# Counting TensorE's instructions in the planner: runs of 96 small products instead of 192, and 12 opening zero products instead of 50

## The chip, the cores and the metric

The kernel runs on one core of one Trainium2 chip. The metric is the device time in microseconds (us), taken as the median of timed runs. The core's engines work from queues of their own: TensorE (PE: matmuls, and PEld: its weight loads), VectorE (DVE), ScalarE (ACT), GpSimd (POOL) and SyncE (SP, which here issues nearly all DMAs). An instruction waits on its queue for the results that it needs, and what stands behind it in the same queue waits too.

## The reference

Two things are computed, one after the other. First a linear attention with a decaying state, step by step over 768 tokens, for 4 batches × 8 heads of width 48:

```python
for t in range(S):
    cur = einsum('bhd,bhe->bhde', u * k[t], v[t])
    y[:, :, t] = einsum('bhd,bhde->bhe', r[t], state + cur)
    state = w[t][..., None] * state + einsum('bhd,bhe->bhde', k[t], v[t])
```

Then a two-layer network on the 3072 × 384 matrix x made of y: h = x @ w_in (384 to 2048), g = h where h >= 1, 0 where h <= -1, (h + 1)² / 4 between, and out = g @ w_out (2048 to 384). All in float32.

## The kernel before, in words

**The network.** The 3072 tokens are cut into 6 blocks of 512 (`WIDE`), and the 2048 hidden columns into 16 groups f of 128. A step is one block and one f. `product_in` (matmuls at line 1272) makes h from x in nine matmuls of 512 columns: three row blocks, each as high × high, high × low and low × high part of numbers split into two float32r halves. The gate follows: Relu and Square on ACT (lines 1084 and 1085), min and max on DVE (1086), the high half on ACT (1088), the low half on DVE (1089). `product_out` (line 1292), nine matmuls again, adds the result into three PSUM banks. h takes one of two spare PSUM banks (`SPARE`, an operation with `grab` takes one, the one that names it in `drop` gives it back). Blocks 0 and 1 start with half steps of 256 columns (`HALVES`), because x of their second half comes later. The last block goes another way (`fast`, matmuls at line 984) that isn't touched.

**The weights** arrive as raw words, one f at a time, and are decoded by ACT (lines 441, 445, 447), POOL or DVE (449) and DVE (451, 454). Line 454 finishes the low half of one f.

**The attention** is done in 12 units u of 64 tokens of every batch, two units to a block. For each, DVE runs a scan forward and one backward over the decays (514 and 509) and scales r and k (585, 535). Then PE issues small products of 64 rows, 64 columns or so, in stretches:
- `among` (line 555): 32 matmuls, r with k inside the unit, one stretch more with u for u < 3; DVE masks the result (561).
- `ktrans` (594): 4 transposes for each of two halves of k, copied by ACT (603).
- `cross` (667): 16 matmuls, r with the old state; u = 0 has none. It holds a spare bank in units 1 to 10, in which the second half of umat is written.
- `umat` (624): 32 matmuls, k with v; DVE makes the new state of it (640, 642, 645).
- `along` (667): the other 16 of r with the state and 32 of the inner part with v, into the same two banks as cross. ACT and DVE then move y out as x in two halves (739, 741); in units 0 and 1 over a spreading product (`spread`, 760).

A float32 matmul of this kind is issued in two passes, each a weight load and a matmul, so one call is four instructions and two matmul records; a float32r one is two instructions and one record.

**The order** of all engines is written out by a planner, class `Plan`. Each operation is added with its engine, cost in us, due time and what it reads and writes. `order` is a list scheduler: it takes the engine that can go first, and on it the ready operation with the smallest key. A result is seen by another engine `HOP` later. `late` runs the same backwards from the end and gives keys; `best` tries 40 orders with shaken keys (`SHAKES`, fixed seed) and keeps the one with the earliest modelled end. `glue` ties operations of PE into a run that nothing may part. `kept_warm` puts products with a tile of zeros (`zeros`, line 403) into pauses of PE that the model sees in the opening. `warm` (line 409) opens PE's queue with `WARM` small zero products, each over one quarter of the array.

The lines that matter most here, from the function `attention`:

```python
run.append(op("PE", 0.6 if glued else 0.8, ..., cross, fresh=not alone, grab=glued))
if glued:
    run.append(multiplied())            # umat
run.append(op("PE", (1.6 if glued else 1.74) if u else 1.27, ..., along, fresh=False))
if glued:
    plan.glue(*run)
```

So in units 1 to 10 (`glued`) cross, umat and along stand in one run. Unit 11 has no umat and isn't glued; unit 0 has no cross.

Of the kernel before, what the change touches and what calls it, by code (L numbers as in the profile page):

```python
# [41 lines left out]
LAG = 2  # L42

FAST = {NB - 1}

WARM = 50

# [15 lines left out]
class Plan:  # L63
# [13 lines left out]
    def add(self, engine, cost, emit, due, reads=(), writes=(), port=False, size=0, fresh=True, first=None, grab=False, uses=(), drop=None):  # L77
# [9 lines left out]
        self.ops.append(dict(e=engine, cost=cost, emit=emit, due=due, deps=deps, port=port, size=size,  # L87
                             fresh=fresh and engine == "PE", touch={*reads, *writes}, first=first, grab=grab, drop=drop, then=None,
                             uses={n} if grab else {*uses, *(() if drop is None else (drop,))}))
        return n  # L90
# [45 lines left out]
    def late(self):  # L136

        ops = self.ops
        users, left = [[] for _ in ops], [0] * len(ops)
        deps = [op["deps"] | {self.extra[n]} if n in self.extra else op["deps"] for n, op in enumerate(ops)]  # L140
        for n in range(len(ops)):
            for m in deps[n]:
                users[m].append(n)
                left[m] += 1
        free, back, since, open_, port = {}, {}, {}, {}, 0.0

        def opened(n):
            op = ops[n]
            since[n] = max((back[m] + (0.0 if ops[m]["e"] == op["e"] and not op["size"] else self.HOP) for m in users[n]), default=0.0)
            since[n] += self.end[n] - self.begin[n] - op["cost"]  # L150
            open_.setdefault(op["e"], []).append(n)

        def ready(n):
            return max(since[n], port) if ops[n]["port"] else since[n]

        for n, k in enumerate(left):
            if not k:
                opened(n)
        while any(open_.values()):
            t, e = min((max(free.get(e, 0.0), min(ready(n) for n in ns)), e) for e, ns in open_.items() if ns)  # L160
            n = max((n for n in open_[e] if ready(n) <= t + 1e-9), key=lambda n: (self.end[n], n))
            open_[e].remove(n)
            back[n] = free[e] = t + ops[n]["cost"]
            if ops[n]["port"]:
                port = back[n]
# [37 lines left out]
    def order(self):  # L203
# [12 lines left out]
        def opened(n):  # L216
            op = ops[n]
            since[n] = max((end[m] + (0.0 if ops[m]["e"] == op["e"] and not ops[m]["size"] else self.HOP) for m in op["deps"]), default=0.0)
# [16 lines left out]
        while any(open_.values()):  # L235
# [27 lines left out]
            begin[n] = t  # L263
            free[e] = end[n] = t + op["cost"] * (2 if e == "PE" and t < RISES else 1)
            if op["port"]:
                port = end[n]
                first.clear()
# [4 lines left out]
            if op["drop"] is not None:  # L272
                spare.append((end[n] + self.HOP, given[op["drop"]], n))
                first["PE"] = None
# [49 lines left out]
def attention_moe(tc, a):  # L324
# [81 lines left out]
    def warm():  # L406
        for n in range(WARM):
            r, c = n % 2 * 64, n // 2 % 2 * 64
            PE.matmul(hp[n % 2][c : c + 64, 0:32], lhsT=zero[r : r + 64, 0:64], rhs=zero[r : r + 64, 0:32], start=True, stop=True)

# [58 lines left out]
    def attention(u, when):  # L469
# [96 lines left out]
        if early:  # L566
            bd = [take(), take()]
            op("PE", 1.27, due, [("ku", 0), ("ku", 1), "nk", *both], [("b", bd[0]), ("b", bd[1])],
               lambda: among(bd, lambda q: ku[:, q]))
            for h in range(2):  # L570
# [19 lines left out]
        def ktrans(q, b):  # L590
# [5 lines left out]
        op("PE", 1.27, due, [("k", slot[0]), ("k", slot[1]), *both], [("b", ba[0]), ("b", ba[1])],  # L596
           lambda: among(ba, lambda q: rk[slot[q]][:, 1]))
        goes_on = u < NU - 1
        for q in (1, 0):
            if goes_on:  # L600
                b = take()
                op("PE", 0.4, due, [("k", slot[q]), "cst"], [("b", b)], lambda q=q, b=b: ktrans(q, b))
                op("ACT", 0.6, due, [("b", b)], [("kt", q)], lambda q=q, b=b: A.copy(
# [45 lines left out]
        def multiplied():  # L649
            return op("PE", 0.94 if glued else 1.27, due, [("kt", 0), ("kt", 1), vk], ukeys, umat, uses=lent.values())  # L650

        def stepped():
            for g in range(2):
                op("DVE", 0.5, due, [ukeys[g], ("ptot", u, 0), ("ptot", u, 1)] + ([("s", old, g)] if u else []), [("s", new, g)],
                   lambda g=g: step(g), drop=lent[0] if glued and g else None)
                if u:
                    op("DVE", 0.47, due, [("ptot", u, 0), ("ptot", u, 1)], [("s", new, g)], lambda g=g: fade(g), port=True)

# [48 lines left out]
        if u:  # L707
            run.append(op("PE", 0.6 if glued else 0.8, due, ss + [vk, ("r", slot[0]), ("r", slot[1])], [("b", by[0]), ("b", by[1])], cross, fresh=not alone,
                          grab=glued))
# [12 lines left out]
        if goes_on:  # L722
            stepped()
# [39 lines left out]
        if alone:  # L763
# [4 lines left out]
            for g in range(2):  # L768
                op("PE", 0.65, due, [("last_f", g), "perm", "nk", "ob"], [("b", by[g])], lambda g=g: spread(g), fresh=False)
        for what in (0,) if alone else (1, 0):  # L770
# [154 lines left out]
    def fast(n, after=()):  # L925
# [13 lines left out]
        hk = op("PE", 2.15, due, [("wh", f), ("wl", f), *xs, *after], [("h", n)],  # L939
                lambda: product_in(nc, bank[plan.given[hk]], f, x[:, 0], x[:, 1], w_hi, w_lo), grab=True)  # L940
        c = 0.6
# [46 lines left out]
        def multiply(late, reads, todo, fresh=False):  # L988
            banks = {("b", PLACE[to][0]): 0 for to, _, _ in todo}
            op("PE", 0.358 * len(todo), (n, -late * STEP - 0.1), reads, list(banks), lambda: accumulate(todo), fresh=fresh)  # L990

# [68 lines left out]
    def products(n, after=()):  # L1060
# [14 lines left out]
        for half in range(2):  # L1075
            if cs.start <= half * UT < cs.stop:
# [3 lines left out]
        step_ops.append(len(plan.ops))  # L1080
        hk = op("PE", 2.15 * k, due, [("wh", f), ("wl", f), *xs, *after], [("h", n)],
                lambda: product_in(nc, hs(), f, x[:, 0, :, cs], x[:, 1, :, cs], w_hi, w_lo), grab=True)
        c = 0.17 + 0.43 * k
# [4 lines left out]
        op("ACT", c, due, [("g", gk)], [("gh", gk)], lambda: nc.scalar.copy(ghs, gs))  # L1088
        op("DVE", 0.15 + 0.5 * k, due, [("g", gk), ("gh", gk)], [("gl", gk)], lambda: nc.vector.tensor_tensor(  # L1089
            out=gls, in0=gs, in1=ghs.bitcast(F32), op=ALU.subtract), port=True)  # L1090
# [5 lines left out]
        def second(n, f, ghs, gls, gk, terms, order=()):  # L1096
            op("PE", 2.15 * k * len(terms) / 9, (n, -LAG * STEP * k), [("gh", gk), ("gl", gk), ("wh", f), ("wl", f)],
               [*({("b", 3 + j): 0 for _, j in terms}), *order], fresh=begin,
               emit=lambda stop=end: product_out(nc, [x[:, cs] for x in acc], f, ghs, gls, w_hi, w_lo, begin, stop, terms))
# [262 lines left out]
```

## Time and profile before

| | us |
|---|---|
| timed runs | 511.04, 511.78, 512.08 |
| median | 511.78 |
| the profiled execution's own time | 510.8 |
| its span (first to last instruction) | 509.2 |
| PE busy in it | 486.8 |
| DVE busy | 367.0 |
| ACT busy | 305.6 |
| POOL busy | 97.0 |
| mean granted TensorE clock | 0.994 |

The profile is of one execution. Its page gives busy times and shares of each engine, the busy share in 40 equal slices of the span (a digit is tenths), the costliest groups of instructions, and DMA queues with packets and megabytes. The list of waits says who waited for whom: us in total, how often, the longest. "issue" there is idle time in which the engine waited for nothing that the profile shows. A row of the timeline has the start in us, the length in us, the engine, the line, the operation, output<-inputs, the shapes, how many instructions are merged in it, and in brackets the idle time of the engine before it and what ended it. A row of the table by stretches gives the stretch, its length, and the busy us of PE, PEld, DVE, ACT and POOL with the number of instructions of each.

### The profile page before, as it was taken

How to read it: one execution, taken by the hardware profiler on the slowest of the kernel's cores; microseconds unless marked ns; L12 is line 12 of the kernel's file. 1: busy time of each engine (PE TensorE's matmuls, PEld its weight loads, DVE VectorE, ACT ScalarE, POOL GpSimd, SP SyncE). 2: the span in 40 equal slices, each digit the busy share in tenths (PEclk: the TensorE clock that was granted, in tenths of full speed). 3: DMA queues.
4: the chain of work that ended last, by engine and by line, in shares of the span. 5: the costliest groups of instructions: out<-in, count | busy, mean ns of one | idle time of the engine just before them, and what ended most of it. 6: DMA issues, size and time to landing. Idle time of an engine off the chain costs nothing. (4 is left out here: it accounts for less than half of the span.)

```text
span 509.2 us, 13264 instructions
## 1 busy us (share of the span) xinstructions
PE 486.8 (96%) x5583; PEld 414.9 (81%) x5583; DVE 367.0 (72%) x631; ACT 305.6 (60%) x628; POOL 97.0 (19%) x80
## 2 busy tenths in 40 slices
PE   7778999999999999998999999999999999999994
PEld 5568988888889998877888887878878878889894
DVE  6899899988798888697963377854248544596653
ACT  4577979888866656565454556454365445575550
POOL 1654414411111111123010010200002402402000
PEclk9899999999999999999999999999999999999998
DMA  8977546245633350444320132400102000010002
GB/s 302 407 277 261 209 149 235 64 126 185 203 126 137 114 173 21 147 130 154 104 84 0 63 131 84 132 1 0 63 1 59 0 1 17 19 45 1 3 0 69
DMA packets 22052, 54.72 MB, mean 107 GB/s; under 512 B 3040, under 2 KB 9184, under 8 KB 21984
## 3 DMA queue, kind: packets, MB, share of 16 engines
q1 hardware_dynamic: 21840, 53.65, 30.6%
q8 instruction: 46, 0.75, 0.6%
q14 instruction: 22, 0.18, 0.1%
q10 hardware_dynamic: 144, 0.13, 0.1%
HBM read 47.09 MB, written 4.72 MB: 102 GB/s over the span
## 5 line engine op out<-in xcount | busy, mean ns | idle before, releaser
L1272 PE MATMUL h<-x,wt 128*128 128x512 f32 (+1 forms) x1035 | 219.4, 359 | 1.8 <-DVE x L739 1.5
L1272 PEld LDWEIGHTS h<-x,wt 128*128 128x128 f32 x1035 | 170.0, 188 | 32.5 <-DVE x L739 1.7
L1292 PE MATMUL acc<-gh,wt 128*128 128x512 f32 (+1 forms) x594 | 129.5, 353 | 0.0
L1292 PEld LDWEIGHTS acc<-gh,wt 128*128 128x128 f32 x594 | 97.6, 188 | 17.0
L1086 DVE SCALAR_TENSOR_TENSOR g<-g,h 128x512 f32<-128x512 f32 (+1 forms) x99 | 57.2, 578 | 70.2 <-ACT g L1085 69.9
L1084 ACT ACTIVATE g<-h 128x512 f32<-128x512 f32 (+1 forms) x99 | 50.9, 515 | 79.0 <-PE h L1272 68.0
L1292 PE MATMUL acc<-gl,wt 128*128 128x512 f32 (+1 forms) x297 | 72.1, 351 | 0.0
L1089 DVE TENSOR_TENSOR gl<-g,gh 128x512 fp32r<-128x512 f32 (+1 forms) x99 | 62.6, 642 | 7.8 <-ACT gh L1088 6.6
L1088 ACT CAST gh<-g 128x512 fp32r<-128x512 f32 (+1 forms) x99 | 52.5, 532 | 17.6 <-DVE g L1086 10.1
L1292 PEld LDWEIGHTS acc<-gl,wt 128*128 128x128 f32 x297 | 50.3, 188 | 8.4
L1085 ACT ACTIVATE g<-g 128x512 f32<-128x512 f32 (+1 forms) x99 | 54.5, 551 | 2.9
L581 POOL TENSOR_TENSOR r<-cst,d 128x512 f32<-128x512 f32 x18 | 19.7, 1113 | 168.5 <-PE bank L667 102.6
L449 POOL TENSOR_SCALAR wraw<-fl 128x768 uint16<-128x768 f32 x13 | 40.0, 3084 | 54.6 <-ACT wraw L447 54.6
L514 DVE TENSOR_TENSOR_SCAN p<-wq,seeds 128x520 f32<-128x520 f32 x24 | 32.3, 1346 | 3.2 <-DMA wq<-in_w 2.4
L573 POOL TENSOR_TENSOR nk<-nk 128x768 f32<-128x768 f32 x9 | 17.3, 1927 | 84.1 <-DMA nk<-in_nk 84.1
L509 DVE TENSOR_TENSOR_SCAN y<-wq,seeds 128x520 f32<-128x520 f32 x24 | 30.5, 1269 | 0.8
L945 DVE SCALAR_TENSOR_TENSOR rk<-rk,h 128x512 f32<-128x512 f32 x16 | 11.0, 687 | 18.3 <-ACT rk L944 18.0
L667 PE MATMUL bank<-r,vn 64*64 64x64 f32 (+1 forms) x768 | 15.4, 223 | 9.1 <-issue 9.1
L667 PEld LDWEIGHTS bank<-r,vn 64*64 64x64 f32 (+1 forms) x768 | 13.5, 135 | 9.9 <-issue 9.9
L942 ACT ACTIVATE rk<-h 128x512 f32<-128x512 f32 x16 | 9.6, 598 | 17.9 <-PE h L1272 17.7
L741 ACT CAST x<-bank 128x384 fp32r<-128x384 f32 x24 | 11.3, 485 | 12.3 <-PE bank L667 11.3
L561 DVE COPY_PREDICATED r<-below,bank 128x512 f32<-128x512 int32 x23 | 16.1, 734 | 3.3 <-PE bank L555 3.3
(198 smaller groups left out, 614.3 us busy)
## 6 DMA issues: line engine op xcount, KB each, us to landing
rk<-in_rk SPq DMA_DIRECT2D x24, 512.0 KB, 4.4
wraw<-in_wbits SPq DMA_DIRECT2D x16, 768.0 KB, 7.1
nk<-in_nk SPq DMA_DIRECT2D x9, 768.0 KB, 4.6
wq<-in_w SPq DMA_DIRECT2D x24, 260.5 KB, 3.0
vn<-in_v SPq DMA_DIRECT2D x12, 384.0 KB, 6.9
fl<-in_w SPq DMA_DIRECT2D x12, 260.0 KB, 2.9
out_y<-g SPq DMA_DIRECT2D x10, 256.0 KB, 2.6
x<-last SPq DMA_DIRECT2D x60, 32.0 KB, 2.5
```

Of the source, the lines that this page charges most:

```text
L449: op(on, 0.62 if f in SIGNS else 3.2, due, [("fl", k)], [("raw", f)], lambda: e.tensor_scalar(out=half(1), in0=s, scalar1=0.0, scalar2=327 ...
L509: V.tensor_tensor_scan(out=y_[:, ::-1], data0=w[:, SEG:0:-1], data1=sv[:, ::-1], initial=0.0, op0=ALU.mult, op1=ALU.add)
L514: V.tensor_tensor_scan(out=pv[:, q].rearrange("p n c -> p (n c)"), data0=w[:, 0:SEG], data1=sv, initial=0.0, op0=ALU.mult, op1=ALU.add,)
L581: op("POOL", 1.1, due, ["d", "cst"], [("R", h)], lambda h=h: G.tensor_tensor(out=r_[h], in0=twice.unsqueeze(1).unsqueeze(1).broadcast_to([ ...
L667: PE.matmul(out=bank[by[g]][HP * half : HP * half + M, lo : lo + C], start=first, stop=False, skip_group_check=True, **kw)
L1084: op("ACT", c, due, [("h", n)], [("g", gk)], lambda: nc.scalar.activation(gs, hs(), AF.Relu, scale=0.5, bias=0.5), uses=[hk])
L1085: op("ACT", c, due, (), [("g", gk)], lambda: nc.scalar.activation(gs, gs, AF.Square))
L1086: op("DVE", 0.13 + 0.53 * k, due, [("h", n)], [("g", gk)], lambda: nc.vector.scalar_tensor_tensor(out=gs, in0=gs, scalar=1.0, in1=hs(), op ...
L1088: op("ACT", c, due, [("g", gk)], [("gh", gk)], lambda: nc.scalar.copy(ghs, gs))
L1089: op("DVE", 0.15 + 0.5 * k, due, [("g", gk), ("gh", gk)], [("gl", gk)], lambda: nc.vector.tensor_tensor(out=gls, in0=gs, in1=ghs.bitcast(F ...
L1272: nc.tensor.matmul(hp, lhsT=wx[f][:, cs], rhs=xt[:, j, :], start=n == 0, stop=n == 8)
L1292: nc.tensor.matmul(o[j], lhsT=wx[f][:, cs], rhs=gt, start=first and i == 0, stop=stop and i == 2, skip_group_check=True)
```

## The change

The planner's model of the machine is made finer and gets a count of PE's instructions.
- Operations of PE carry `code`, the number of their instructions: 128 for among and umat, 64 for cross, 192 for along (128 in unit 0), 8 for ktrans, 12 for spread, 18 for a product. In `order`, `issued` keeps how many instructions PE has been given and when. An operation with more than 64 may start only so that its last instruction comes `FETCH` = 3.9 us after the one that stands `BLOCK` = 256 before it.
- cross and umat are still glued, along is not: it is an operation of its own that other products may precede. The state's DVE operations are added ahead of along.
- `after` replaces the single `HOP`: 0.2 us behind PE, 0.12 behind DVE and ACT, 0.15 behind POOL and SP; on ACT an instruction may begin 0.03 before the one ahead ends. Several costs are set anew.
- `warm` issues 12 zero products of 128 columns instead of 50 of 32.

What is computed for the output is the same; the order of the instructions is worked out anew by the same search.

```diff
-WARM = 50
+WARM = 12
...
     HOP = 0.15
+    HOPS = {"PE": 0.2, "DVE": 0.12, "ACT": 0.12, "POOL": 0.15, "SP": 0.15}
+    OVERLAP = {"ACT": 0.03}
+    BLOCK, FETCH = 256, 3.9
+
+    def after(self, m, n):
+
+        a, b = self.ops[m], self.ops[n]
+        if a["e"] == b["e"] and not a["size"]:
+            return 0.03 if a["e"] in self.OVERLAP else 0.0
+        return self.HOPS[a["e"]]
...
+        issued = [(0, -99.0, 0.0)]
+
+        def fetched(code):
+            at = issued[-1][0] + code - self.BLOCK
+            for had, t, each in reversed(issued):
+                if had <= at:
+                    return t + (at - had) * each + self.FETCH
+            return 0.0
+
...
+            if ops[n]["code"] > 64:
+                t = max(t, fetched(ops[n]["code"]) - ops[n]["cost"])
...
+            if e == "PE":
+                had = issued[-1][0]
+                if op["code"]:
+                    issued[-1] = had, t, op["cost"] / op["code"]
+                    issued.append((had + op["code"], t + op["cost"], 0.0))
+                first["PE"] = None
...
-            free[e] = end[n] = t + op["cost"] * (2 if e == "PE" and t < RISES else 1)
+            end[n] = t + op["cost"] * (2 if e == "PE" and t < RISES else 1)
+            free[e] = end[n] - self.OVERLAP.get(e, 0.0)
...
-            PE.matmul(hp[n % 2][c : c + 64, 0:32], lhsT=zero[r : r + 64, 0:64], rhs=zero[r : r + 64, 0:32], start=True, stop=True)
+            PE.matmul(hp[n % 2][c : c + 64, 0:128], lhsT=zero[r : r + 64, 0:64], rhs=zero[r : r + 64, 0:128], start=True, stop=True)
...
-            return op("PE", 0.94 if glued else 1.27, due, [("kt", 0), ("kt", 1), vk], ukeys, umat, uses=lent.values())
+            return op("PE", 1.07 if glued else 1.27, due, [("kt", 0), ("kt", 1), vk], ukeys, umat, uses=lent.values(), code=128)
...
-                op("ACT", 0.35, due, [("b", by[g])], [("look", g)], lambda g=g: A.copy(look[0:1, g : g + 1], bank[by[g]][0:1, 0:1]))
+                op("ACT", 0.15, due, [("b", by[g])], [("look", g)], lambda g=g: A.copy(look[0:1, g : g + 1], bank[by[g]][0:1, 0:1]))
         if glued:
-            run.append(multiplied())
-        run.append(op("PE", (1.6 if glued else 1.74) if u else 1.27, due, ss + [("R", 0), ("R", 1), vk, ("r", slot[0]), ("r", slot[1])],
-                      [("b", by[0]), ("b", by[1])], along, fresh=False))
-        if glued:
-            plan.glue(*run)
-        elif goes_on:
+            plan.glue(*run, multiplied())
+            stepped()
+        op("PE", 1.74 if u else 1.27, due, ss + [("R", 0), ("R", 1), vk, ("r", slot[0]), ("r", slot[1])],
+           [("b", by[0]), ("b", by[1])], along, fresh=False, code=192 if u else 128)
+        if goes_on and not glued:
             multiplied()
-        if goes_on:
             stepped()
```

In the same way the costs of cross (0.6 to 0.64), of the state's steps (0.5 to 0.55 and 0.47 to 0.57), of the products (2.15 to 2.1) and of a few others are set anew.

More of the change, by code (lines that the diff above doesn't have):

```diff
@@ L75, in __init__, with add @@
         self.given, self.extra = {}, {}
-    def add(self, engine, cost, emit, due, reads=(), writes=(), port=False, size=0, fresh=True, first=None, grab=False, uses=(), drop=None):
+    def add(self, engine, cost, emit, due, reads=(), writes=(), port=False, size=0, fresh=True, first=None, grab=False, uses=(), drop=None, code=0):
         deps = {self.writer[x] for x in (*reads, *writes) if x in self.writer}
@@ L87, in add @@
         self.ops.append(dict(e=engine, cost=cost, emit=emit, due=due, deps=deps, port=port, size=size,
-                             fresh=fresh and engine == "PE", touch={*reads, *writes}, first=first, grab=grab, drop=drop, then=None,
+                             fresh=fresh and engine == "PE", touch={*reads, *writes}, first=first, grab=grab, drop=drop, then=None, code=code,
                              uses={n} if grab else {*uses, *(() if drop is None else (drop,))}))
@@ L148, in opened @@
             op = ops[n]
-            since[n] = max((back[m] + (0.0 if ops[m]["e"] == op["e"] and not op["size"] else self.HOP) for m in users[n]), default=0.0)
+            since[n] = max((back[m] + self.after(n, m) for m in users[n]), default=0.0)
             since[n] += self.end[n] - self.begin[n] - op["cost"]
@@ L162, in late @@
             open_[e].remove(n)
-            back[n] = free[e] = t + ops[n]["cost"]
+            back[n] = t + ops[n]["cost"]
+            free[e] = back[n] - self.OVERLAP.get(e, 0.0)
             if ops[n]["port"]:
-                port = back[n]
+                port = free[e]
             for m in deps[n]:
@@ L217, in opened @@
             op = ops[n]
-            since[n] = max((end[m] + (0.0 if ops[m]["e"] == op["e"] and not ops[m]["size"] else self.HOP) for m in op["deps"]), default=0.0)
+            since[n] = max((end[m] + self.after(m, n) for m in op["deps"]), default=0.0)
             open_.setdefault(op["e"], []).append(n)
         forced, given, extra = {}, {}, {}
+        issued = [(0, -99.0, 0.0)]
[5 more added lines that the diff above has]
+            return 0.0
         spare = [(0.0, b, None) for b in SPARE]
@@ L263, in order @@
             begin[n] = t
-            free[e] = end[n] = t + op["cost"] * (2 if e == "PE" and t < RISES else 1)
+            end[n] = t + op["cost"] * (2 if e == "PE" and t < RISES else 1)
+            free[e] = end[n] - self.OVERLAP.get(e, 0.0)
             if op["port"]:
-                port = end[n]
+                port = free[e]
                 first.clear()
@@ L272, in order @@
             if op["drop"] is not None:
-                spare.append((end[n] + self.HOP, given[op["drop"]], n))
+                spare.append((end[n] + self.HOPS[e], given[op["drop"]], n))
                 first["PE"] = None
@@ L649, in multiplied @@
         def multiplied():
[L650 removed]
+            return op("PE", 1.07 if glued else 1.27, due, [("kt", 0), ("kt", 1), vk], ukeys, umat, uses=lent.values(), code=128)
         def stepped():
             for g in range(2):
[L654 removed]
+                op("DVE", 0.55, due, [ukeys[g], ("ptot", u, 0), ("ptot", u, 1)] + ([("s", old, g)] if u else []), [("s", new, g)],
                    lambda g=g: step(g), drop=lent[0] if glued and g else None)
                 if u:
[L657 removed]
+                    op("DVE", 0.57, due, [("ptot", u, 0), ("ptot", u, 1)], [("s", new, g)], lambda g=g: fade(g), port=True)
         begun = set()
@@ L707, in attention @@
         if u:
-            run.append(op("PE", 0.6 if glued else 0.8, due, ss + [vk, ("r", slot[0]), ("r", slot[1])], [("b", by[0]), ("b", by[1])], cross, fresh=not alone,
-                          grab=glued))
+            run.append(op("PE", 0.64 if glued else 0.8, due, ss + [vk, ("r", slot[0]), ("r", slot[1])], [("b", by[0]), ("b", by[1])], cross, fresh=not alone,
+                          grab=glued, code=64))
             if glued:
@@ L938, in fast @@
         step_ops.append(len(plan.ops))
-        hk = op("PE", 2.15, due, [("wh", f), ("wl", f), *xs, *after], [("h", n)],
-                lambda: product_in(nc, bank[plan.given[hk]], f, x[:, 0], x[:, 1], w_hi, w_lo), grab=True)
+        hk = op("PE", 2.1, due, [("wh", f), ("wl", f), *xs, *after], [("h", n)],
+                lambda: product_in(nc, bank[plan.given[hk]], f, x[:, 0], x[:, 1], w_hi, w_lo), grab=True, code=18)
         c = 0.6
@@ L989, in multiply @@
             banks = {("b", PLACE[to][0]): 0 for to, _, _ in todo}
-            op("PE", 0.358 * len(todo), (n, -late * STEP - 0.1), reads, list(banks), lambda: accumulate(todo), fresh=fresh)
+            op("PE", 0.351 * len(todo), (n, -late * STEP - 0.1), reads, list(banks), lambda: accumulate(todo), fresh=fresh, code=6 * len(todo))
         n0, f0, f1 = n - odd, f - odd, f - odd + 1
@@ L1080, in products @@
         step_ops.append(len(plan.ops))
-        hk = op("PE", 2.15 * k, due, [("wh", f), ("wl", f), *xs, *after], [("h", n)],
-                lambda: product_in(nc, hs(), f, x[:, 0, :, cs], x[:, 1, :, cs], w_hi, w_lo), grab=True)
+        hk = op("PE", 2.1 * k, due, [("wh", f), ("wl", f), *xs, *after], [("h", n)],
+                lambda: product_in(nc, hs(), f, x[:, 0, :, cs], x[:, 1, :, cs], w_hi, w_lo), grab=True, code=18)
         c = 0.17 + 0.43 * k
@@ L1088, in products @@
         op("ACT", c, due, [("g", gk)], [("gh", gk)], lambda: nc.scalar.copy(ghs, gs))
-        op("DVE", 0.15 + 0.5 * k, due, [("g", gk), ("gh", gk)], [("gl", gk)], lambda: nc.vector.tensor_tensor(
+        op("DVE", 0.17 + 0.54 * k, due, [("g", gk), ("gh", gk)], [("gl", gk)], lambda: nc.vector.tensor_tensor(
             out=gls, in0=gs, in1=ghs.bitcast(F32), op=ALU.subtract), port=True)
@@ L1096, in second @@
         def second(n, f, ghs, gls, gk, terms, order=()):
-            op("PE", 2.15 * k * len(terms) / 9, (n, -LAG * STEP * k), [("gh", gk), ("gl", gk), ("wh", f), ("wl", f)],
-               [*({("b", 3 + j): 0 for _, j in terms}), *order], fresh=begin,
+            op("PE", 2.1 * k * len(terms) / 9, (n, -LAG * STEP * k), [("gh", gk), ("gl", gk), ("wh", f), ("wl", f)],
+               [*({("b", 3 + j): 0 for _, j in terms}), *order], fresh=begin, code=2 * len(terms),
                emit=lambda stop=end: product_out(nc, [x[:, cs] for x in acc], f, ghs, gls, w_hi, w_lo, begin, stop, terms))
```

8 lines of the change are left out of this document (4 added, 4 removed).

## The prediction

> **What bounds the kernel now.** I read the page first, then the waits of TensorE (PE), then PE's timeline around each wait.
>
> ```profile
> span 509.2 us, 13264 instructions
> PE 486.8 (96%) x5583; PEld 414.9 (81%) x5583; DVE 367.0 (72%) x631; ACT 305.6 (60%) x628; POOL 97.0 (19%) x80
> PE   7778999999999999998999999999999999999994
> DVE  6899899988798888697963377854248544596653
> PEclk9899999999999999999999999999999999999998
> q8 instruction: 46, 0.75, 0.6%
> ```
>
> PE is busy for 96% of the span; from the fifth slice on (51 us) it is close to full, so from there time is won only by shortening PE's own row. PE idles 509.2 − 486.8 = 22.4 us. The two rows of the 40 slices show a second limit: in slices 3 to 9 VectorE (DVE) is at 8 or 9 tenths too. What PE waits for:
>
> ```profile
> PE bank L667 <- issue: 9.1, 6, 2.7
> PE h L409 <- POOL zero L388: 2.8, 1, 2.8
> PE h L1272 <- DVE x L739: 1.5, 1, 1.5
> ```
>
> The largest entry waits for no engine and no DMA: six pauses, "issue", all at line 667, the products that write y. In the order of time they are these (the bracket is the idle time before the row; x is the number of matmuls left after the pause):
>
> ```profile
> 18.98 1.10 PE L667 MATMUL bank<-r,vn 64*48 64x64 f32 x30 [2.67 <-issue]
> 41.69 0.67 PE L667 MATMUL bank<-r,vn 64*48 64x64 f32 x33 [1.70 <-issue]
> 71.84 0.57 PE L667 MATMUL bank<-r,vn 64*64 64x64 f32 x21 [1.09 <-issue]
> 128.44 0.50 PE L667 MATMUL bank<-r,vn 64*64 64x64 f32 x18 [1.16 <-issue]
> 151.46 0.75 PE L667 MATMUL bank<-r,vn 64*64 64x64 f32 x37 [0.93 <-issue]
> 240.03 0.56 PE L667 MATMUL bank<-r,vn 64*64 64x64 f32 x19 [1.53 <-issue]
> ```
>
> They belong to units u = 0, 1, 2, 3, 4 and 7. A unit from 1 to 10 issues cross, umat and along as one run of 32 + 64 + 96 = 192 matmul records; each record has a weight load of its own (5583 of both on the page), so 384 instructions. Here is u = 7, which pauses, and then u = 8, which doesn't:
>
> ```profile
> 235.72 0.69 PE L667 MATMUL bank<-rk,st 64*64 64x64 f32 x32
> 237.16 0.66 PE L667 MATMUL bank<-rk,st 64*64 64x64 f32 x32
> 237.64 0.87 PE L667 MATMUL bank<-r,vn 64*64 64x64 f32 x45
> ...
> 293.22 0.70 PE L667 MATMUL bank<-rk,st 64*64 64x64 f32 x32
> 293.74 0.20 PE L624 MATMUL bank<-vn,kt 64*64 64x48 f32 x1
> 294.66 0.66 PE L667 MATMUL bank<-rk,st 64*64 64x64 f32 x32
> 295.14 1.11 PE L667 MATMUL bank<-r,vn 64*64 64x64 f32 x64
> 296.18 1.66 PE L1292 MATMUL acc<-gh,wt 128*128 128x512 f32 x6
> ```
>
> I read the pause as instructions that have not arrived. The instruction queue row has 46 packets for 0.75 MB, about 16 KB each, and 2 × 5583 = 11166 PE instructions over 46 packets are some 243 each, so one packet carries about 256 instructions of 64 bytes. In u = 7 the pause follows 32 + 64 + 32 + 45 = 173 records; 256 instructions (128 records) before the first one that is late is the 13th or so of the 64 umat records, which by even spacing ran at about 236.4. From there to 240.03 are 3.6 us. A block that lies wholly in a run is used up in about 2 us (192 records take 296.18 − 293.22 = 2.96 us), and the next one is late. A run of 384 can hold a whole block or miss it: (384 − 256) / 256 is a half, and 5 of the 10 long runs pause.
>
> [...]
>
> **The change part by part.**
>
> *Long run cut in two (u = 1 to 10).* cross + umat stays glued, 192 instructions; along, again 192, may start only when the planner's count has its last instruction fetched: 256 back in the count plus 3.9 us. Right behind umat that is 1.8 us or so after umat's end, so the planner puts a product between, 2.10 us (the plain pitch of nine records, below). The tightest block then holds 46 instructions of umat, the product's 18 and all of along: about 0.3 + 2.2 + 1.5 = 4.0 us, longer than the 3.6 measured. I take all five pauses as gone: 1.70 + 1.09 + 1.16 + 0.93 + 1.53 = **−6.41 us**. Lower bound of the gain: 0, if they move elsewhere.
>
> *What the cut costs.* Unit 11 already issues its cross apart from its along, so its rows price it, against a plain product and against u = 8 above:
>
> ```profile
> 99.75 1.56 PE L1292 MATMUL acc<-gh,wt 128*128 128x512 f32 x6
> 101.85 0.39 PE L1272 MATMUL h<-x,wt 128*128 128x512 f32 x1
> ...
> 418.00 0.69 PE L667 MATMUL bank<-rk,st 64*64 64x64 f32 x32
> 418.62 2.36 PE L1272 MATMUL h<-x,wt 128*128 128x512 f32 x9
> 420.82 1.56 PE L1292 MATMUL acc<-gh,wt 128*128 128x512 f32 x6
> 423.01 0.69 PE L667 MATMUL bank<-rk,st 64*64 64x64 f32 x32
> 424.57 1.66 PE L1292 MATMUL acc<-gh,wt 128*128 128x512 f32 x6
> ```
>
> A plain product takes 2.10; the one after the small group 420.82 − 418.62 = 2.20, the one before it 423.01 − 420.82 = 2.19. cross alone lasts 0.62 against 293.74 − 293.22 = 0.52, along alone 1.56 against 296.18 − 294.66 = 1.52. Together 0.10 + 0.09 + 0.10 + 0.04 = 0.33 us for a cut, and ten of them are **+3.3 us**. Where along comes to stand beside another small product the cost is less; bounds 1.5 to 3.3, and I take 3.3 because unit 11 is the same step.
>
> *u = 0 and the opening zeros.* The opening zeros go from 50 × 2 records to 12 × 2, (100 − 24) × 2 = 152 instructions less, which moves every later block border back against the work. The 2.67 us pause came after 34 of along's 64 records; 152 instructions further on lies behind the end of along, so I take it as gone, and the planner's count also holds along back until its block is there. What does that win?
>
> ```profile
> 20.12 0.43 ACT L765 COPY ob<-bank 128x128 f32<-128x128 f32 x2 [3.98 <-PE bank L667]
> 23.26 1.01 DVE L454 TENSOR_TENSOR wt<-fl,wt 128x768 fp32r<-128x768 f32 x1 [0.61 <-ACT wt L441]
> 26.54 1.01 DVE L739 TENSOR_TENSOR x<-bank,x 128x384 fp32r<-128x384 f32 x2
> ```
>
> ScalarE (ACT) waited 3.98 us for along, but DVE, which must give x and the first weights before the first product, lost only 0.61 us to it, and at 26.54 it took x up without waiting. So **−0.6 us**; bounds 0 and −2.7. That the 24 zeros of 128 columns take another time than the 100 of 32 costs nothing: a 3.2 us stretch of filling zeros stands behind them. [...]
>
> ```profile
> 5.69 3.23 PE L403 MATMUL bank<-zero 128*128 128x512 f32 x6
> ```
>
> *Costs and hops in the planner* (0.2 behind PE, 0.12 behind DVE and ACT, ACT overlapping 0.03, the look copies 0.15 for 0.35) move no instruction by themselves; they make a new order out of the same search. I price them at 0, bounds −1.5 and +1.5, the size of a pause.
>
> *How much of the early gain reaches the end.* Up to 105 us the terms are −0.6, −(1.70 − 0.33) and −(1.09 − 0.33), together −2.7. But there DVE has no room:
>
> ```profile
> 75.00:102.00 27.00, 27.00 (x122) 21.91 (x121) 26.20 (x38) 24.37 (x39) 12.35 (x4) 1.00 0.45 160
> 87.15 4.36 PE L1272 MATMUL h<-x,wt 128*128 128x512 f32 x18
> 86.26 0.93 DVE L454 TENSOR_TENSOR wt<-fl,wt 128x768 fp32r<-128x768 f32 x1
> 102.00:500.00 398.00, 393.74 (x4164) 336.20 (x4163) 271.75 (x489) 227.10 (x484) 52.97 (x52) 1.00 0.23 74
> ```
>
> From 75 to 102 us DVE is busy 26.20 of 27.00. The weights of a block are finished by line 454, in the order of use; the one of the 86.26 row ends at 87.2 and its product starts with the second nine of the 87.15 row, at 89.25: 2.0 us of slack. PE can come 2.0 us earlier and then waits for weights. I let **−2.0** of the −2.7 through. Behind 102 us DVE is busy 68% and PE 99%, so what is won there stays: pauses −(1.16 + 0.93 + 1.53) = −3.62, eight cuts +2.64, **−1.0**.
>
> **Sum:** −2.0 − 1.0 = −3.0 us. The profiled execution took 510.8 us (span 509.2 and 1.6 around it), which becomes 507.8. The median of the three timed runs, 511.78, lies 1.0 above it; against that I predict **508.8 us**.
>
> **Rivals.**
>
> 1. *Everything passes.* The planner finds other DVE work to put off and nothing waits for weights, u = 0 gives all it can: −6.41 − 2.67 + 3.3 = −5.8, 506.0 us. For it: the order is made anew. Against it: DVE's 26.20 of 27.00.
> 2. *The early part gives nothing*, DVE sets the pace to 105 us, only −1.0 is left: 510.8 us.
> 3. *The change doesn't do what it says*: the pauses do not hang on the length of a run and stay, so the ten cuts are all that is added: 511.8 + 3.3 = 515.1 us. [...] Against it: all six pauses lie deep in stretches of small products, none elsewhere.
> 4. *The lent bank (slower).* cross borrows one of the two PSUM banks of the h products and gives it back when DVE has taken umat's second half. Before, along kept PE on other banks for 1.5 us meanwhile; now a product follows at once, and the one after it needs the lent bank. It decides where DVE takes more than a product, 2.1 us, to give it back.
>
> ```profile
> 38.92 0.63 PE L667 MATMUL bank<-rk,st 64*48 64x64 f32 x32
> 41.45 0.55 DVE L642 TENSOR_TENSOR st<-h,st 128x384 f32<-128x384 f32 x1
> ```
>
> In u = 1 umat ends about 38.92 and the step on the lent bank at 42.00, 3.1 us; if the four early units all waited 3.1 − 2.1 = 1.0 us, 508.8 + 4.0 = 512.8 us. Against it: second products, which need no such bank, can go between.
>
> **How the numbers follow.** Forecast 0.45, rival 1 0.13, rival 2 0.18, rival 3 0.07, rival 4 0.08, and 0.09 for a new order that costs the 1.5 us and more by itself (511 to 513). The forecast's own range, with the cut at 1.5 to 3.3 and the order at ±1.5, is 506.3 to 510.3. About 0.2% (1.0 us) can be told from no change: faster means below 510.8, slower above 512.8. The forecast (0.45) and rival 1 are faster, rival 2 stands on the border (0.10 faster, 0.08 same), rival 3 slower, rival 4 half and half, the new order 0.04 same and 0.05 slower: faster 0.68, same 0.16, slower 0.16. The range 505.3 to 512.4 leaves out rival 3, part of rival 4 and the ends.
>
> **What would show it.** The waits of PE should have no "issue" at line 667 behind u = 0 and at most 1 us in all; along should be a group of 96 records with a product ahead of it, and that product's pitch 2.2 rather than 2.1. PE's gaps between 60 and 105 us should name DVE at line 454 or the gate if the slack is used up. Line 409 should have 24 records. I am wrong if pauses of a microsecond turn up in runs of 96, if the first 50 us win more than 2 us, or if PE begins to wait for DVE at lines 642 or 1086 behind the units.

## The result, and the profile after

| | before, us | changed, us | ratio, 95% interval |
|---|---|---|---|
| first comparison, 7 runs of each | 510.98 | 507.71 | 0.9947 [0.9923, 0.9971] |
| second comparison, another session | 510.01 (16 runs) | 509.18 (11 runs) | 0.9973 [0.9956, 0.9990] |

The changed kernel is faster, by 0.5% in the first comparison and 0.3% in the second. The forecast was 508.8. The profiled execution of the changed kernel took 508.99 us, the longest of its seven, so its span lies about 1 us above a usual one. From its page:

```profile
span 507.3 us, 13117 instructions
PE 492.1 (97%) x5525; PEld 417.2 (82%) x5525; DVE 368.3 (73%) x631; ACT 299.9 (59%) x628; POOL 100.4 (20%) x80
PE   6989999999999999999999999999999999999995
DVE  6999989988888797835888435987333486697753
PEclk9989999999999999999999999999999999999998
q8 instruction: 45, 0.74, 0.6%
```

PE idles 507.3 − 492.1 = 15.2 us where it idled 22.4, but it is busy for 5.3 us more: the idle time went and about three quarters of it came back as busy time. This is all that PE waits for in the changed kernel (line numbers are 27 to 29 higher now):

```profile
PE h L438 <- POOL zero L417: 2.8, 1, 2.8
PE bank L584 <- DVE rk L614: 1.8, 1, 1.8
PE bank L623 <- DVE rk L564: 1.6, 2, 1.4
PE h L1299 <- DVE g L1113: 0.8, 2, 0.5
PE bank L584 <- ACT nk L554: 0.6, 1, 0.6
PE h L1299 <- DVE r L590: 0.4, 1, 0.4
PE bank L584 <- DVE x L766: 0.4, 1, 0.4
```

The entry of 9.1 us for "issue" is gone, at unit 0 too. What took its place are waits, mostly for VectorE: beside the first row 5.6 us, of which all but 1.2 us end before 32 us. In PE's timeline, unit 8, where the run was whole before, reads:

```profile
307.06 2.25 PE L1299 MATMUL h<-x,wt 128*128 128x512 f32 x9
309.25 0.69 PE L696 MATMUL bank<-rk,st 64*64 64x64 f32 x32
...
310.80 1.66 PE L1319 MATMUL acc<-gh,wt 128*128 128x512 f32 x6
...
313.09 0.69 PE L696 MATMUL bank<-rk,st 64*64 64x64 f32 x32
...
314.65 2.36 PE L1299 MATMUL h<-x,wt 128*128 128x512 f32 x9
316.85 0.63 PE L1319 MATMUL acc<-gh,wt 128*128 128x512 f32 x2
```

A product of 313.09 − 310.80 = 2.29 us stands between cross + umat (1.55) and along (1.56), and the product before it takes 2.19, the one behind 2.20. Against plain 2.10, and against 1.44 and 1.52 in the whole run, that is 0.19 + 0.11 + 0.04 + 0.09 + 0.10 = 0.53 us; a whole run costs its two neighbours 0.09 and 0.10 too, so the cut costs 0.34 us.

To compare kernels whose order differs, I counted for each profiled execution the time that PE has lost up to a moment: the time, less each matmul so far at its plain pitch (0.233 us for 512 columns, 0.117 for 256, 1.10 us for 64 records of among and so on, zeros at nothing). It is good to some half a microsecond.

```
us lost by PE up to            50 us   105 us   the last matmul   (which ends at)
before                          26.7     28.3        38.5            502.7
changed                         25.8     26.5        36.7            501.0
changed, second profile         26.8     27.6        37.1            501.4
cut and count alone             26.2     27.5        34.8            499.0
changed, 50 opening zeros       25.1     25.8        34.1            498.2
   second profile               25.3     26.0        34.5            498.5
before, 8 opening zeros         27.4     28.7        37.6            501.8
changed, long runs, 20 zeros    25.3     25.5        36.2            500.3
```

Where two kernels issue the same products in the same order and differ in their opening zeros alone, no count is needed: the start of each matmul in one timeline can be set against the same matmul in the other. "Row by row" below means that.

### The profile page after: what moved, and what is told of

Its sections match the earlier page's. It is cut to its first block, busy times and chain, and to the rows that moved or that the text cites. A ratio compares the mean times of both kernels' runs of the same rounds, so it can differ in the third digit from the quotient of the medians.

```text
span 507.3 us, 13117 instructions
## 1 busy us (share of the span) xinstructions
PE 492.1 (97%) x5525; PEld 417.2 (82%) x5525; DVE 368.3 (73%) x631; ACT 299.9 (59%) x628; POOL 100.4 (20%) x80
## 5 line engine op out<-in xcount | busy, mean ns | idle before, releaser
L1299 PEld LDWEIGHTS h<-x,wt 128*128 128x128 f32 x1035 | 169.9, 188 | 32.6 <-DVE g L1113 1.8
L478 POOL TENSOR_SCALAR wraw<-fl 128x768 uint16<-128x768 f32 x13 | 43.3, 3354 | 50.1 <-ACT wraw L476 38.7
L543 DVE TENSOR_TENSOR_SCAN p<-wq,seeds 128x520 f32<-128x520 f32 x24 | 30.1, 1254 | 3.0 <-DMA wq<-in_w 2.1
L564 DVE TENSOR_TENSOR rk<-rk,y 128x512 f32<-128x512 f32 x24 | 18.0, 750 | 0.9 <-ACT nk L554 0.7
L696 PEld LDWEIGHTS bank<-rk,st 64*64 64x64 f32 (+1 forms) x704 | 12.2, 133 | 6.7 <-issue 5.0
```

The lines of the kernel that those rows point to most:

```text
L478: op(on, 0.62 if f in SIGNS else 3.2, due, [("fl", k)], [("raw", f)], lambda: e.tensor_scalar(out=half(1), in0=s, scalar1=0.0, scalar2=327 ...
L543: V.tensor_tensor_scan(out=pv[:, q].rearrange("p n c -> p (n c)"), data0=w[:, 0:SEG], data1=sv, initial=0.0, op0=ALU.mult, op1=ALU.add,)
L564: op("DVE", 0.69, due, ["y"], [("k", s)], lambda q=q: V.tensor_tensor(out=parts(q, 1), in0=parts(q, 1), in1=y_.rearrange("p (n c) -> p n c ...
L1299: nc.tensor.matmul(hp, lhsT=wx[f][:, cs], rhs=xt[:, j, :], start=n == 0, stop=n == 8)
```

## The experiments

**Is it the place of a block of 256 in a run, or the unit's work?** Counted in weight loads and matmuls of the kernel before, the first matmul behind each of the six pauses (units 0, 1, 2, 3, 4, 7) stands at 189, 185, 183, 179, 179 and 167 modulo 256. If this is a border (the place where one block of 256 ends and the next begins) whose next block has not arrived in time, moving the stream moves the pauses to other units. The number of opening zeros does that and leaves the order of everything else as it was.

```diff
-WARM = 50
+WARM = 18
...
-  PE.matmul(hp[n % 2][c : c + 64, 0:32], ..., rhs=zero[r : r + 64, 0:32], ...)
+  PE.matmul(hp[n % 2][c : c + 64, 0:128], ..., rhs=zero[r : r + 64, 0:128], ...)
```

> The kernel before with 18 opening zero products of 128 columns instead of 50 of 32, nothing else: every later instruction of PE stands 128 places (half a block of 256) earlier in the stream, the order is the same. Theory (a block of 256 arrives too late when one block border lies in the first third of a run of 384 and the next one in its end): counted in the stream, the six pauses of before all stand at the same place modulo 256, give or take 12; moved by 128, units 1, 2, 3, 4 and 7 have no pause, and units 5, 8, 9 and 10 have one of 0.9 to 1.7 us, unit 6 at most 0.6 at its very end; unit 0's pause goes. Sum of issue waits at the lines of the run 4 to 6.5 us, time within 2.5 us below the kernel before. Rival (the pause comes from the work of the unit, not from its place in the stream): the same six pauses at units 0, 1, 2, 3, 4 and 7, 9.1 us.

Its list of waits for issue, and the rows behind its pauses in PE's timeline:

```profile
PE bank L667 <- issue: 4.9, 5, 1.6
175.81 0.45 PE L667 MATMUL bank<-r,vn 64*64 64x64 f32 x13 [1.64 <-issue]
218.27 0.33 PE L667 MATMUL bank<-r,vn 64*64 64x64 f32 x2 [0.91 <-issue]
296.14 1.04 PE L667 MATMUL bank<-r,vn 64*64 64x64 f32 x54 [0.47 <-issue]
322.12 0.46 PE L667 MATMUL bank<-r,vn 64*64 64x64 f32 x15 [0.93 <-issue]
387.28 0.57 PE L667 MATMUL bank<-r,vn 64*64 64x64 f32 x21 [0.90 <-issue]
```

These are units 5, 6, 8, 9 and 10, and units 1 to 4 and 7 run through. In the stream the pauses stand at 175, 169, 161, 161 and 157 modulo 256. The sizes were not all as expected: unit 8 paused 0.47 us (0.9 at least was expected), unit 6 0.91 (0.6 at most), and unit 0 kept a pause of 0.68 us, in its umat, where none was expected. But the rival falls: the same work in the same order pauses or not by its place.

The places drift only because this count leaves out the other instructions in TensorE's queue, some 50, nearly all waits for semaphores. Counted with them, all these pauses end at place 193 or 194 modulo 256, and so do all 35 pauses above 0.25 us in the fourteen profiles of this study.

The time did not follow: 511.85 us, ratio 1.0031 [1.0010, 1.0052], where up to 2.5 us less was expected. Row by row (its profiled execution took 513.77 us) it stands level with the kernel before at 105 us, 0.1 us behind, although pauses of 5.5 us in units 0 to 2 are gone. PE waited for x in the opening instead, ran 3.4 us at half clock from 29.5 us (64 records of among took 1.89 us there, 1.16 at 33.9 us), and at 89 us met this:

```profile
PE h L1272 <- DVE g L1086: 1.4, 1, 1.4
```

Behind 105 us it loses 2.7 us more: five pauses stand there instead of three, and at 125.8 us PE waits 1.2 us longer for kt.

The same with 8 zeros (`WARM = 8`):

> The kernel before with 8 opening zero products of 128 columns: 168 places earlier in the stream, the same order, all long runs still whole. Theory: only unit 8 has its borders so that it pauses (border 73 instructions into the run), once, 0.9 to 1.7 us; issue waits fall from 9.1 to 1.7 us or less, with no cost of a cut, so the time falls 3.5 to 6 us below the kernel before. Rival (place in the stream is nothing): six pauses, the time of the kernel before within 1 us.

```profile
293.30 0.74 PE L667 MATMUL bank<-r,vn 64*64 64x64 f32 x34 [0.90 <-issue]
383.94 0.27 PE L667 MATMUL bank<-r,vn 64*64 64x64 f32 x1 [1.52 <-issue]
```

Unit 8 pauses as expected; unit 10 as well, one record before its end, because my count of places left out the other instructions in the queue, some 35 of them by then. Three smaller ones were not expected either, 0.32 us in unit 3, 0.28 behind unit 5 and 0.68 in the umat of unit 0, and the waits for issue at line 667 are 2.7 us, not 1.7. 508.52 us, ratio 0.9958 [0.9942, 0.9975]: this kernel, which cuts nothing and counts nothing, wins as much as the change, though less than the 3.5 to 6 us that I expected. Row by row it is 0.4 us behind the kernel before at 105 us and 0.9 ahead at the end (in a profiled execution 1.4 us above its median).

With 12 zeros, the opening part of the change alone:

> The opening part of the change alone: the kernel before with 12 opening zero products of 128 columns (152 places earlier). Theory: unit 8 pauses (border 57 in), units 5 and 10 have their second border 381 to 383 into the 384, so a short one of some 0.6 us each at the end or none; unit 0's goes. Issue waits 1 to 3 us instead of 9.1, time 3 to 5 us below the kernel before: then most of what the change won would have come from the 152 instructions, not from the cut. Rival (the cut is what wins): within 1 us of the kernel before.

```profile
PE bank L667 <- issue: 4.4, 4, 1.3
PE h L409 <- POOL zero L388: 2.8, 1, 2.8
PE h L1272 <- ACT x L741: 2.7, 1, 2.7
PE h L1272 <- DVE x L739: 1.8, 1, 1.8
```

Four pauses instead of six at line 667, in units 5, 8, 9 and 10, 4.4 us instead of 9.1 (and 0.63 in the umat of unit 0), and 510.50 us, ratio 1.0003 [0.9986, 1.0021]: nothing won, where I expected 3 to 5 us. Row by row it is 0.3 us ahead of the kernel before at 105 us and 0.2 at the end: behind 105 us four pauses took the place of three of 3.6 us. In the opening PE now waits 2.7 us for x and then runs at half clock; the stretch from 26 to 33 us, first of before and then of this kernel (the columns behind POOL are the clock, the DMA share and GB/s):

```profile
26.00:33.00 7.00, 5.04 (x136) 4.23 (x139) 6.88 (x11) 5.13 (x11) 1.32 (x1) 1.00 0.87 317
```

```profile
26.00:33.00 7.00, 4.97 (x75) 4.34 (x76) 5.55 (x9) 3.99 (x9) 0.00 (x0) 0.51 0.83 313
```

75 matmuls in about the same busy time, at a granted clock of 0.51, where before had 136.

The three kernels also price a pause. Where units 3, 4 and 7 do not pause, the row moves up by 1.37, 1.14 to 1.15 and 1.73 to 1.74 us, some 0.2 us more than the idle time of 1.16, 0.93 and 1.53.

**The cut and the count alone**, in the kernel before, with its opening, hops and other costs:

```diff
-        if glued:
-            run.append(multiplied())
-        run.append(op("PE", (1.6 if glued else 1.74) if u else 1.27, ..., along, fresh=False))
-        if glued:
-            plan.glue(*run)
+        if glued:
+            plan.glue(*run, multiplied())
+            stepped()
+        op("PE", 1.74 if u else 1.27, ..., along, fresh=False, code=192 if u else 128)
...
+            if ops[n]["code"] > 64:
+                t = max(t, fetched(ops[n]["code"]) - ops[n]["cost"])
```

> The kernel before with the cut and the count of instructions alone: along no longer tied to cross and umat, the 256-back-plus-3.9-us rule, their costs (cross 0.64, umat 1.07, along 1.74); the opening (50 zero products of 32 columns), the hops and all other costs stay as before. The order is worked out anew. Theory: the cut is what wins: no pause of a microsecond behind unit 0, ten cuts of 0.33 us, 2 to 4 us below the kernel before. Rival (the new hops and costs of the planner win, or the opening does): within 1 us of the kernel before.

507.66 us, ratio 0.9951 [0.9936, 0.9966]. Its waits for issue are 1.8 us, of which 1.46 stand at unit 0 and 0.29 at unit 1. The cut and the count by themselves give what the whole change gives; on this chip their median is 1.5 us below the changed kernel's.

**The change without the cut**: along tied to cross and umat again, the count made void.

```diff
-            plan.glue(*run, multiplied())
-            stepped()
+            run.append(multiplied())
+        run.append(op("PE", (1.6 if glued else 1.74) if u else 1.27, ..., along, fresh=False, ...))
+        if glued:
+            plan.glue(*run)
...
-            if ops[n]["code"] > 64:
+            if ops[n]["code"] > 640:
```

> The changed kernel with along tied to cross and umat again and the count of instructions without effect: new hops, costs and opening alone, order anew. Counted in its stream, the border falls 93, 81 and 67 instructions into the runs of units 3, 4 and 7. Theory: those three pause, 0.9 to 1.7 us each, no other unit from 1 to 10 does (unit 0 a part of a microsecond); no cut is paid, so the time is within 1.5 us of the changed kernel (3.6 us of pauses against 3.3 us of cuts). Rival (any run of 384 tends to pause): five or more pauses and 3 us or more above the changed kernel.

```profile
135.66 0.46 PE L696 MATMUL bank<-r,vn 64*64 64x64 f32 x14 [0.88 <-issue]
157.05 0.57 PE L696 MATMUL bank<-r,vn 64*64 64x64 f32 x22 [1.10 <-issue]
258.80 0.73 PE L696 MATMUL bank<-r,vn 64*64 64x64 f32 x33 [1.36 <-issue]
```

Units 3, 4 and 7, and no other behind unit 0 (which pauses 0.76 us in its umat): the three that the count of places named. The time is 512.08 us, ratio 1.0039 [1.0024, 1.0055], 2.9 us above the changed kernel on the same chip, more than the 1.5 I allowed: 3.3 us of pauses stand against 3.4 us of cuts, and the rest are single waits of this order (1.2 us for DVE at 120.7, 0.5 for a gate at 369.5 among them).

**The change with the cut, but without the count** (only the second edit of the diff above):

> The changed kernel with the count of instructions without effect, the cut kept: the planner may put along right behind umat, and does so in units 1 and 7; in the others a product stands between because its key comes first. Theory: unit 7 (border 53 in) pauses 0.9 to 1.7 us, unit 1 (border 199 in) does not; unit 0's stretch pauses up to 1 us; the time is 0 to 1.5 us above the changed kernel, so the cut itself does most and the count little. Rival (the count does it): 2 us or more above the changed kernel.

```profile
263.79 0.81 PE L696 MATMUL bank<-r,vn 64*64 64x64 f32 x41 [1.53 <-issue]
```

Unit 7 pauses and unit 1 does not, as the places say. But 513.65 us, ratio 1.0055 [1.0039, 1.0071], is 4.5 us above the changed kernel; I had expected 0 to 1.5, and by its number the rival is nearer. The pause accounts for 1.5 of it; the rest is again the order: 3.3 us of waiting for ACT at 27.9 with half clock behind it (mean granted clock of the span 0.986, in the changed kernel's 0.993), and 1.7 us in five waits for gates. The count moves more than the one product that it forces.

**The opening.** The changed kernel with the 50 zeros of before, on two chips, and the changed kernel itself beside the other runs:

> The changed kernel with its opening of before, 50 zero products of 32 columns (152 places later), the rest of its order the same. Theory: runs of 192 with a product between hold no whole block, so no pause of a microsecond appears wherever the borders lie, and the time stays within 1 us of the changed kernel, about 3 us below the kernel before; in the opening unit 0 may pause up to 1 us, which VectorE's work covers. Rival (the opening is what wins): 2 us or more above the changed kernel.

> The changed kernel with 50 opening zero products of 32 columns once more, on another chip. If the 12 short ones cost time in the opening: 0.6 to 1.0% below the kernel before, and no stretch of half TensorE clock before 500 us. If the first result was chance: 0.3 to 0.5% below, as the changed kernel itself.

> The changed kernel once more, beside the other runs on one chip. Both theories: 0.3 to 0.8% below the kernel before.

With 50 zeros: 506.48 us, ratio 0.9916 [0.9899, 0.9934], and 506.98 us, ratio 0.9932 [0.9917, 0.9948]; as changed: 0.9947 and 0.9973 (the table on top). This is the best kernel of the study. So the opening part of the change costs 0.3 to 0.4%, although unit 0 pauses 1.2 to 1.3 us with 50 zeros and not with 12. Half clock alone doesn't explain it: the changed kernel had a stretch of 3.4 us at half clock from 32.3 us (mean granted clock from 32 to 36 us: 0.57), its second profile two (10.1 and 34.0 us; 0.75 from 32 to 36 us), the first of the kernels with 50 zeros none (1.00), but the second had one at 32.6 us (0.58), which I had not expected, and was as fast.

Nor does the loss stand in the opening alone. Against the first kernel with 50 zeros, row by row, the changed kernel is 0.6 us behind at 105 us and 2.8 at the end; its second profile 1.7 and 3.2. The rest, 2.3 and 1.6 us, goes mostly around 122, 150 and 367 us, where PE waits for DVE, twice for a gate. At the first and the last of these, in the changed kernel's first profile, ACT has just waited for a store of output that reads g, 1.01 and 3.44 us; with 50 zeros it waits for none there. First the changed kernel, then with 50 zeros:

```profile
ACT g L1111 <- DMA out_y<-g: 6.5, 4, 3.4
```

```profile
ACT g L1111 <- DMA out_y<-g: 2.1, 3, 1.7
```

In the second profiles these are 7.9 and 2.1 us. Why the stores land later with 12 zeros stays open.

Is it the time that the zeros take? 12 zeros of 256 columns:

```diff
-  PE.matmul(hp[n % 2][c : c + 64, 0:128], ..., rhs=zero[r : r + 64, 0:128], ...)
+  PE.matmul(hp[n % 2][c : c + 64, 0:256], ..., rhs=zero[r : r + 64].unsqueeze(1).broadcast_to([64, 2, 128]), ...)
```

> The changed kernel with its 12 opening zero products 256 columns wide instead of 128: the same places in the stream, the same order, only about 1.5 us more of opening work for TensorE. Theory (the 24 records of 128 columns end at 4.3 us, the queue runs dry before the first transposes and the clock falls back to half later): the gap before the first transposes (1.4 to 1.8 us) shrinks by about 1.5 us, the time comes within 0.3% of the kernel with 50, 0.6 to 1.0% below the kernel before. Rival (the 152 places of the stream make the difference, not the time): as the changed kernel, 0.3 to 0.5% below.

507.97 us, ratio 0.9945 [0.9924, 0.9965]. The gap before the first transposes shrank to 0.8 us, by 0.6 to 1.0 rather than 1.5, and the interval holds both theories. A pause that the changed kernel does not have adds to it:

```profile
PE h L1299 <- issue: 0.9, 1, 0.9
```

It stands at 39.3 us in unit 1, inside the product between umat and along, at place 194 modulo 256. Without a stretch at half clock in the opening (mean granted clock of the span 0.996, in the changed kernel's 0.993) this kernel is 1.0 us ahead of the changed one at 36 us, row by row, and this pause loses it again. What makes the opening slower stays open.

**What an order is worth.** The kernel with 50 zeros and another seed (`SEED = 2`):

> The changed kernel with 50 opening zero products and another seed for the search: another order of the same worth to the planner. Both theories: no pause behind unit 0; how far its time lies from that of the first seed, 0 to 2 us to either side, is what an order made anew is worth by itself.

508.14 us, ratio 0.9958 [0.9937, 0.9978], 1.2 us above the first seed on the same chip, with no pause of a microsecond behind unit 0 (0.45 us in unit 1).

**Long runs, but placed.** If the place decides, a run need not be cut where the border is well. The changed kernel with along tied on in units 1 to 10 and freed from the count, and 20 zeros of 128 columns:

```diff
-WARM = 12
+WARM = 20
...
+LONG = {1, 2, 3, 4, 5, 6, 7, 8, 9, 10}
...
-            if ops[n]["code"] > 64:
+            if ops[n]["code"] > 64 and not ops[n].get("free"):
...
+        if u in LONG:
+            plan.ops[last_op]["free"] = True
+            plan.glue(*run, last_op)
```

> The changed kernel's costs, hops and count, but along tied to cross and umat again in units 1 to 10 and free of the count, and 20 opening zero products of 128 columns, chosen so that counted in the stream no block border falls 8 to 127 instructions into a long run, but for unit 10 (123). Theory: at most one pause, of 0.3 to 0.9 us, in unit 10; no cut is paid, so about 3.3 - 0.6 = 2.7 us below the changed kernel with 50 opening products, if the new order costs nothing, and 0.7 to 1.6% below the kernel before. Rival (runs of 384 pause wherever they lie): three or more pauses, not below the changed kernel.

Its one pause, and two rows of the timeline at 122 us:

```profile
402.88 0.33 PE L697 MATMUL bank<-r,vn 64*64 64x64 f32 x5 [1.21 <-issue]
...
121.69 0.66 ACT L1118 ACTIVATE g<-h 128x256 f32<-128x256 f32 x2 [2.70 <-DMA out_y<-g]
123.16 1.32 PE L1306 MATMUL h<-x,wt 128*128 128x256 f32 x9 [2.91 <-DVE g L1120]
```

Ten runs of 384 with one pause, in unit 10, where it was expected (1.21 us, expected 0.3 to 0.9). The time, 508.98 us with runs from 505.96 to 512.03, ratio 0.9980 [0.9953, 1.0006], won nothing: in this order a gate waits 2.70 us on ACT until the store of an output block has left the tile g, and PE behind it 2.91 us. That wait alone is as large as the 2.7 us that the uncut runs were to save.

## Why the prediction was right, and where it was not

**The pauses (predicted −6.41 us, all gone): shown.** They are instructions that come late. The pauses sit at one place modulo 256, move to other units with the stream, and come back in three units and in one where two kernels restore long runs. In the trace's DMA records one packet of 16384 bytes of the instruction queue belongs to each border, in order, and it lands 1.3 to 1.6 us before each of the 35 pauses ends (for unit 7 at 238.59, the pause ends at 240.03). No block in the fourteen profiles is entered sooner than 1.26 us after its packet has landed.

The estimate of 3.6 us for a block was good enough behind unit 1: there no run cut by a product paused, in seven profiles, and the shortest block of the changed kernel lasted 4.2 us. It is no rule. The kernel before uses up a block in 2.4 us at 215 us without a pause, because the next packet had landed 5.2 us earlier; with the 12 wide zeros PE pauses 0.89 us behind a block of 6.5 us. What decides is when the packet begins, 2.3 to 2.9 us before the end of each pause; what starts it, no run here shows. No packet begins more than some 300 instructions ahead of its block (297 at most in the profile of before, 301 in the changed kernel's). Rival 3, in which the pauses stay, falls.

**The price of a cut (0.33 us): right**, 0.34 measured in unit 8.

**The early part (−2.0 of −2.7 us let through): near in size in one profile, wrong in reason.** By the lost time at 105 us it gave −1.8 and −0.7 us in two profiles. I had PE wait for weights; in the list of waits of the changed kernel no weight appears. What took the gain lies before 50 us: lost time there fell only by 0.9 us in one profile and not at all in the other, where the terms for units 0 and 1 were 0.6 + 1.37. The failed step is "That the 24 zeros of 128 columns take another time than the 100 of 32 costs nothing". I named the 3.2 us of filling zeros, but they run on behind the shorter opening at once, so that PE waits 1.4 to 1.8 us before the first transposes. That wait is not itself the price: the transposes wait for DVE and start at 9.35 and 9.25 us, against 9.20 and 8.97 with 50 zeros. By the kernels with 50 zeros the part costs 0.3 to 0.4%, before and behind 105 us. That DVE has no room before 105 us was right, more so than I allowed: in the three kernels that keep the order, 5.5 us of early pauses are gone and the row at 105 us moves by −0.3 to +0.4 us. One of the waits that take it back, 1.44 us for the gate at 89 us, stands at the very product whose slack I had reckoned. The pause of unit 0 was worth next to nothing, as argued; but a shorter opening also moves the border ahead of it, and in those three kernels unit 0 pauses 0.6 to 0.7 us in its umat.

**The late part (−1.0): smaller**, 0 and −0.7 us by the lost time between 105 us and the last matmul. The cuts were as priced. The pauses were worth more, some 0.2 us each, and with 50 zeros the late part gave −1.9 and −1.7 us. The difference are the waits around 122, 150 and 367 us, 0.3 to 0.5 us each in PE's list. At the first of these, ACT too waits for a store of output to leave g:

```profile
121.81 0.97 PE L1299 MATMUL h<-x,wt 128*128 128x256 f32 x6 [0.30 <-DVE g L1113]
121.91 0.39 ACT L1111 ACTIVATE g<-h 128x256 f32<-128x256 f32 x1 [1.01 <-DMA out_y<-g]
```

**The hops and costs (0, ±1.5).** Between the kernel with cut and count alone (0.9951) and the changed one with 50 zeros (0.9916, 0.9932) the gain is 0.2 to 0.35%, but a seed moves an order by 1.2 us too, so I cannot say that the new costs earned it. The bound of 1.5 us was too narrow for the order: without the count it came out 3 us worse beside its pause. Of the rivals, 1 and 2 lie on either side of what happened; 4, the lent bank, shows in no list of waits of the changed kernel (line 642 of before does not appear there; the gate, line 1086 of before, does, twice, 0.8 us in all, but not behind a unit).

**The sum** of −3.0 us stands against −3.3 and −0.8 us between the medians, −2.7 and −1.4 by the ratios. That the first comparison comes so near is partly luck: by the lost time the two profiled executions won 1.8 and 1.4 us. The 508.8 stands between the two measured medians, from a base of three runs that lay 0.8 us above the median of all seven.

## What to carry to other kernels

Count instructions, not only microseconds: here a stretch of 256 small TensorE instructions used up in some 2 us can leave the next block of code late, by 0.3 to 1.7 us behind unit 0, and a single large product in the stretch hid it everywhere behind unit 1. Whether a given stretch paused depended in these runs on its place in the stream, so an edit anywhere ahead of it, such as a few opening instructions, moves time that seems to have nothing to do with it: compare the pauses before crediting the edit. And where a search makes the order anew, price its chance as well (1.2 us by one seed here), or undo the parts one by one with the order held.

## What the runs showed that I had not expected

- Eight opening zero products for 50, which move the stream by 168 instructions and leave the order as it was, won 0.42% [0.25, 0.58] of the time, as much as the planner's new count. With 12 and 18 nothing was won: other units paused.
- Half clock in the opening (granted 0.50) lasted 3.41 us in the profile of before, from 18.5 us, near the end of the pause of 2.67 us at unit 0, and 3.41 us in the changed kernel's, from 32.3 us, 0.6 us behind a wait of 1.84 us for DVE. With 12 zeros alone it filled the stretch from 26 to 33 us (granted 0.51 there), around waits of 2.66 us for ACT and 1.80 us for DVE.
- A store of output that leaves its tile late held ACT for 2.70 us and PE for 2.91 us in the middle of a kernel that is bound by PE; the kernel before has 6.1 us of such waits on ACT, the changed one 6.5 and 7.9, with 50 zeros 2.1.
